# Interleaving the two heads of a block-diagonal attention tile over the partitions

## The chip, the cores and the metric

The kernel runs on one core of one Trainium2 chip. The metric is the device time of one execution in microseconds (us); a lower time is better. The core has five engines that matter here: PE (TensorE, matmul; PEld is its loading of weights), DVE (VectorE), ACT (ScalarE), POOL (GpSimd) and SP (SyncE, which issues most DMAs). Sixteen DMA engines carry out what SP and ACT issue.

## The reference, cut to what matters

```python
# B, H, S, D = 4, 8, 768, 64; chunks of 32 queries, 16 keys to the left, 8 to the right, 8 memory keys
q_c    = q[:, :, c_start:c_end]                           # 32 queries of a chunk
k_full = concatenate([mem_k, k[:, :, l_start:r_end]])     # 8 + 56 = 64 keys (fewer at the two ends of S)
v_full = concatenate([mem_v, v[:, :, l_start:r_end]])
scores = 0.125 * (q_c @ k_full.T);  scores -= max(scores)
a      = exp(scores);  a /= sum(a) + 1e-9
out[:, :, c_start:c_end] = a @ v_full
# then on all 3072 tokens, x is 3072 x 512:
h  = x @ w_in                                             # 512 x 1024
ln = layernorm(h * softmax(h)) * g_ln
x2 = ln @ w_out                                           # 1024 x 512
y  = leaky_relu(x2 @ w_in2, 0.01) @ w_out2                # 512 x 2048, 2048 x 512
```

## The kernel before, in words

The weights arrive as 64-bit floats, which the kernel decodes on the chip into pairs of float32 halves. The first 340 us or so hold attention and the first feed-forward layer; the rest holds the second one, which the change does not touch.

Attention works on 24 tiles of 128 tokens of one batch entry. A tile holds 8 heads, taken as 4 pairs (`hp`), and 4 chunks (`c`) of 32 tokens. For each pair and chunk one matmul computes the scores of both heads at once: the contraction runs over 128 partitions, 64 for each of the two heads, and the moving operand (`kbd`) is block diagonal. Its shape is `[128, 2, 4, 4, 64]`, where the second index `j` says for which head of the pair the 64 key columns are. For `j = 0` the lower 64 partitions hold the keys of head 0 and the upper 64 partitions hold zeros; for `j = 1` it is the other way round. The values (`vbd`) are laid out the same way, with 64 keys of each head on the partitions. The zeros are written once, by two memsets of a buffer, and the loads of all later tiles leave them alone. There are four such buffers: `kbd` and `vbd` (zeroed by DVE, used for tile 0 and for tiles 2 and on) and `k1` and `v1` (zeroed by POOL, used for tile 1 alone).

One tile goes through `s_scores` (16 matmuls, line 204; row maxima on DVE, lines 213 and 214), `s_exp` (8 ACT instructions of 128 x 64 into `p`, line 221), `s_pt` (4 transposes of 128 x 128 on PE, line 234, and a copy, line 238), `s_pv` (16 matmuls, line 246, and the division by the row sum, line 251), and `s_xt` (4 transposes, line 260, and the split into halves, lines 263 and 266). `s_h` and what follows is the first feed-forward layer (line 91 is the helper that records its matmuls, line 351 the second product).

Every load of `kbd` or `vbd` is two DMAs of 256 KB from SP (line 185), one for each `j`, with 64 partitions of 4 KB each. A load of `q` is one DMA of 256 KB over 128 partitions (line 179), a load of raw weights one DMA of 512 KB over 128 partitions (lines 97 and 99).

At the start SP issues loads in an order written out by hand, `LOADS` (w0 to w7 are the eight pieces of the first weight matrix, raw):

```python
LOADS = "q0 k0 w0 w1 k1 q1 w5 v0 w3 w2 v1 w7 w4 g w6".split()
STEPS = "a10100a10ab03a21b22a14a223b34353bbb55447564667656777"
```

`STEPS` is the order in which DVE, ACT and POOL take the steps of the first two tiles (`a`, `b`) and of the decoding of w0 to w7 (`0` to `7`). Line 109 is the first step of a decoding and waits for the raw weights. After that the framework's planner sets the order of the instructions on each engine by modelled times, until the second feed-forward layer, which is written out by hand again.

Of the kernel before, what the change touches and what calls it, by code (L numbers as in the profile page):

```python
# [9 lines left out]
F32 = mybir.dt.float32  # L10
F32R = mybir.dt.float32r
U32 = mybir.dt.uint32
AF = mybir.ActivationFunctionType
# [26 lines left out]
def tile_kernel(  # L40
# [13 lines left out]
    P = 128  # L54
# [12 lines left out]
    SCALE = 0.125  # L67
# [10 lines left out]
    ident = const.tile([P, P], F32, name="ident")  # L78
# [83 lines left out]
    p1 = satt.enter_context(tc.tile_pool(name="p1", bufs=1, side="right"))  # L162
# [2 lines left out]

    def kv_tile(pool, name, eng):
        t = pool.tile([P, 2, 4, 4, 64], F32, name=name)
        eng.memset(t[0:64, 1], 0.0)
        eng.memset(t[64:128, 0], 0.0)
        return t  # L170

    warm = sm.tile([P, 1], F32, name="warm")
    nc.scalar.activation(warm, mhalf, AF.Exp)
    kbd = kv_tile(p1, "kbd", nc.vector)
    vbd = kv_tile(p1, "vbd", nc.vector)

    def load_q(i):
# [3 lines left out]

    def load_kv(i, dst, src):
        for j in range(2):
            sl = slice(64 * j, 64 * j + 64)
            nc.sync.dma_start(
                out=dst[sl, j], in_=src[i, sl].rearrange("p (h c k) -> p h c k", h=4, c=4)
            )
        return dst

    def load_tile(i):  # L190
        return load_q(i), load_kv(i, kbd, kw), load_kv(i, vbd, vw)
# [7 lines left out]
    def s_scores(i, q, k):  # L199
        sc = ps_att.tile([P, 8, 64], F32, name="att")  # L200
        for hp in range(4):
            for c in range(4):
                cs = slice(32 * c, 32 * c + 32)
                nc.tensor.matmul(  # L204
                    sc[cs, 2 * hp : 2 * hp + 2, :], q[:, hp, cs], k[:, :, hp, c, :],
                    start=True, stop=True,
                )
        if i % TPB == 0:
            nc.vector.memset(sc[0:32, :, 8:24], NEG)
        if i % TPB == TPB - 1:  # L210
            nc.vector.memset(sc[96:128, :, 56:64], NEG)
        nms = sm.tile([P, 8], F32, name="nms")
        nc.vector.tensor_reduce(out=nms, in_=sc, op=ALU.max, axis=AX.X, negate=True)
        nc.vector.tensor_scalar_mul(nms, nms, SCALE)  # L214
        return sc, nms

    def s_exp(sc, nms):
        p = p1.tile([P, 8, 64], F32, name="p")
        rs = sm.tile([P, 8], F32, name="rs")
        for h in range(8):  # L220
            nc.scalar.activation(  # L221
                p[:, h], sc[:, h], AF.Exp, bias=nms[:, h : h + 1], scale=SCALE,
                accum_out=rs[:, h : h + 1],
            )
        return p, rs
# [5 lines left out]
    def s_pt(p):  # L231
        ptp = ps_tr.tile([P, 4, P], F32, name="tr")
        for hp in range(4):
            nc.tensor.transpose(
                ptp[:, hp], p[:, 2 * hp : 2 * hp + 2].rearrange("p h k -> p (h k)"), ident
            )
        pt = pa.tile([P, 4, P], F32, name="pt")
        nc.vector.tensor_copy(pt, ptp)
        return pt
# [120 lines left out]
    def att_steps(i, ld):  # L360
        sc, nms = s_scores(i, ld[0], ld[1])
        yield
        p, rs = s_exp(sc, nms)
        yield
        s_rs(rs)
        pt = s_pt(p)
        yield
        x = s_pv(pt, ld[2], rs)
        yield
        hl, low = s_xt(x)  # L370
        xs.append(hl)
        yield
        low()
        yield

    def w1_raw(u):
        hf, kk = divmod(u, KD)
        return load_raw(w1[kk * P : (kk + 1) * P, hf * 1024 : (hf + 1) * 1024], sraw)

    k1 = kv_tile(st, "k1", nc.gpsimd)  # L380
    v1 = kv_tile(st, "v1", nc.gpsimd)
    got = {}
    for d in LOADS:
        if d == "g":
            nc.sync.dma_start(out=g_sb, in_=g_ln.rearrange("(k p) -> p k", p=P))
            continue
        n = int(d[1])
        if d[0] == "q":
            got[d] = load_q(n)
        elif d[0] == "k":  # L390
            got[d] = load_kv(n, (kbd, k1)[n], kw)
        elif d[0] == "v":
            got[d] = load_kv(n, (vbd, v1)[n], vw)
        else:
            got[d] = w1_raw(n)
# [37 lines left out]
    for i in range(NTILE + 1):  # L433
        a = i + 2
        b, t = divmod(i, TB)
# [4 lines left out]
        if att:  # L440
            p, rs = s_exp(*s_scores(a, ld[0], ld[1]))
            s_rs(rs)
# [10 lines left out]
        if att:  # L453
            pt = s_pt(p)
        if so is not None:
            j = i - 1
# [34 lines left out]
    spx, sxr, sxt, sl, sr, sq, sd, sg, s4 = (ExitStack() for _ in range(9))  # L491
# [64 lines left out]
    for i in range(NTILE + 1, NTILE + LAG):  # L556
        j = i - LAG
# [211 lines left out]
    for n, (q, v) in enumerate(units):  # L769
# [8 lines left out]
        k = n - NA  # L778
# [51 lines left out]
    hp = s4.enter_context(tc.tile_pool(name="hp", bufs=2, side="right", reuse_waits="tile"))  # L830
# [24 lines left out]
    for n, (v, s, k) in enumerate(steps):  # L855
        h, l = halves.pop(n)
        if s == 0 and k == 0:
            acc = {c: [ps.tile([P, BT], F32, name=c) for e in range(2)] for c in "ABC"}
            A, B, C = (acc[c] for c in "ABC")
# [105 lines left out]
```

## Time and profile before

| what | value |
|---|---|
| median of 3 runs | 866.36 us (865.71 to 875.55) |
| profiled execution | 871.68 us, of which 869.9 us are the span from the first to the last instruction |
| mean granted TensorE clock | 0.994 of full speed |
| busy share of the span | PE 95%, PEld 76%, DVE 74%, ACT 54%, POOL 7% |
| DMA | 190.95 MB, mean 220 GB/s |

The profiled execution is 5.3 us longer than the median; sums made from the trace are set against the profiled one and then moved by that amount.

### The profile page before, as it was taken

The numbers are of one execution on the slowest core, as the hardware profiler recorded it, in microseconds if no ns is written. First come the engines' busy times: TensorE is split into PE (matmuls) and PEld (weight loads), VectorE is DVE, ScalarE is ACT, GpSimd is POOL, SyncE is SP. The second block draws the span as 40 slices with busy tenths as digits, with TensorE's granted clock in tenths as the row PEclk, the third lists the DMA queues.
The fourth block names the chain that finished last, engine by engine and source line by source line (L and its number), as shares of the span: only waits on it lengthen the run. The fifth ranks groups of instructions, "written<-read, shape, count | busy, mean of one in ns | idle before, by whom it ended". The sixth has DMA issues, their size and how long they took to land.

```text
span 869.9 us, 13633 instructions
## 1 busy us (share of the span) xinstructions
PE 827.6 (95%) x4960; PEld 658.1 (76%) x4960; DVE 643.4 (74%) x1145; ACT 472.2 (54%) x1067; POOL 56.6 (7%) x63
## 2 busy tenths in 40 slices
PE   3789999999999999996999999999999999999998
PEld 2457777777777778784887888788877888888886
DVE  4788986777877778758889843856579869758673
ACT  2477864455554544536556644677657535544541
POOL 2233420000000000000000000000000010010001
PEclk9999999999999999998999999999999999999999
DMA  8756777968697763572688756377777466646542
GB/s 227 180 161 195 206 204 227 282 198 260 201 287 226 234 212 140 194 269 88 244 324 325 281 222 236 139 289 294 269 287 282 146 221 206 198 161 227 197 145 97
DMA packets 69891, 190.95 MB, mean 220 GB/s; under 512 B 8000, under 2 KB 32064, under 8 KB 65856
## 3 DMA queue, kind: packets, MB, share of 16 engines
q1 hardware_dynamic: 56864, 175.14, 60.4%
q10 hardware_dynamic: 12960, 14.95, 5.5%
q8 instruction: 39, 0.64, 0.3%
q14 instruction: 28, 0.23, 0.1%
HBM read 129.24 MB, written 60.82 MB: 218 GB/s over the span
## 4 chain that ended last, share of the span: by engine, by line
PE 74%; DVE 12%; DMA 6%; ACT 4%; issue 2%; POOL 1%; SPq 0%; ACTq 0%; DVEq 0%; POOLq 0%
PE C L654 24%; PE B L654 14%; PE x2p L351 12%; PE A L654 10%; PE h L91 9%; DMA raw<-in_w 2%; PE att L246 2%; PE att L204 2%; DMA x2d<-x2s 1%; DMA ring<-gd 1%; DVE so L290 1%; ACT p L221 1%; DMA kbd<-in_kw 1%; DVE m L124 1%; PE tr L260 1%
## 5 line engine op out<-in xcount | busy, mean ns | idle before, releaser
L351 PE MATMUL x2p<-lhl,w2h 128*128 128x512 f32 x384 | 127.3, 406 | 0.5 <-ACT x2s L357 0.5
L654 PE MATMUL C<-xP,L 128*128 128x512 f32 x384 | 97.4, 395 | 7.5 <-ACT u L683 5.9
L654 PEld LDWEIGHTS C<-xP,L 128*128 128x128 f32 x384 | 72.4, 190 | 24.9 <-ACT u L683 6.7
L351 PEld LDWEIGHTS x2p<-lhl,w2h 128*128 128x128 f32 x384 | 70.1, 189 | 16.8 <-issue 2.0
L351 PE MATMUL x2p<-lhl,w2l 128*128 128x512 f32 x192 | 77.5, 404 | 0.0
L221 ACT ACTIVATE p<-att,nms 128x64 f32<-128x64 f32 x192 | 57.4, 322 | 23.5 <-DVE nms L214 23.4
L91 PE MATMUL h<-w1h,xh 128*128 128x512 f32 x168 | 68.7, 409 | 1.5 <-ACT w1h L133 1.5
L91 PE MATMUL h<-w1l,xh 128*128 128x512 f32 x168 | 67.5, 402 | 2.3 <-POOL w1l L134 2.3
L654 PE MATMUL C<-h,L 128*128 128x512 f32 x192 | 67.0, 390 | 0.0
L91 PE MATMUL h<-w1h,xl 128*128 128x512 f32 x168 | 66.7, 397 | 0.0
L765 DVE TENSOR_TENSOR ring<-ring,h 128x512 fp32r<-128x512 f32 x96 | 61.8, 685 | 3.7 <-ACT h L764 3.1
L680 ACT ACTIVATE g<-g 128x512 f32<-128x512 f32 x72 | 45.1, 627 | 26.0 <-DVE g L699 20.0
L295 ACT ACTIVATE e<-so,nmu 128x1024 f32<-128x1024 f32 x24 | 27.7, 1154 | 57.1 <-DVE nmu L293 56.6
L764 ACT ACTIVATE h<-ring 128x512 fp32r<-128x512 f32 x72 | 39.8, 621 | 31.7 <-DMA ring<-gd 22.8
L654 PE MATMUL B<-xP,L 128*128 128x512 f32 x192 | 49.7, 395 | 0.2 <-DVE g L709 0.2
L699 DVE TENSOR_TENSOR g<-B,u 128x512 f32<-128x512 f32 x23 | 15.9, 690 | 42.2 <-PE B L654 42.2
L764 ACT ACTIVATE h<-t2k 128x512 fp32r<-128x512 f32 x48 | 28.7, 628 | 33.1 <-DVE t2k L757 18.6
L654 PEld LDWEIGHTS B<-xP,L 128*128 128x128 f32 x192 | 36.5, 191 | 8.6 <-DVE g L709 0.6
L351 PEld LDWEIGHTS x2p<-lhl,w2l 128*128 128x128 f32 x192 | 36.2, 189 | 7.8 <-issue 1.0
L654 PEld LDWEIGHTS C<-h,L 128*128 128x128 f32 x192 | 36.0, 188 | 7.9 <-DVE u L879 0.4
L221 ACT ACTIVATION_READ_ACCUMULATOR p<-att,nms 128x1 f32 x192 | 41.3, 215 | 0.0
L91 PEld LDWEIGHTS h<-w1h,xh 128*128 128x128 f32 x168 | 31.8, 189 | 11.6 <-issue 3.2
(183 smaller groups left out, 1908.3 us busy)
## 6 DMA issues: line engine op xcount, KB each, us to landing
ring<-gd SPq DMA_DIRECT2D x48, 768.0 KB, 4.0
gd<-g SPq DMA_DIRECT2D x24, 1024.0 KB, 5.1
raw<-in_w SPq DMA_DIRECT2D x32, 512.0 KB, 5.3
L<-w3f SPq DMA_DIRECT2D x14, 896.0 KB, 4.7
kbd<-in_kw SPq DMA_DIRECT2D x46, 256.0 KB, 4.6
vbd<-in_vw SPq DMA_DIRECT2D x46, 256.0 KB, 4.3
lnd<-sl SPq DMA_DIRECT2D x16, 512.0 KB, 3.4
lt<-lnd ACTq DMA_DIRECT2D x64, 128.0 KB, 2.8
```

The lines of the kernel that those rows point to most:

```text
L91: nc.tensor.matmul(ps, a, b, start=(i == 0), stop=(i == 3 * n - 1))
L124: nc.vector.scalar_tensor_tensor(out=mu, in0=raw[:, :, 1], scalar=0x80000000, in1=mu, op0=ALU.bitwise_and, op1=ALU.bitwise_or,)
L204: nc.tensor.matmul(sc[cs, 2 * hp : 2 * hp + 2, :], q[:, hp, cs], k[:, :, hp, c, :], start=True, stop=True,)
L221: nc.scalar.activation(p[:, h], sc[:, h], AF.Exp, bias=nms[:, h : h + 1], scale=SCALE, accum_out=rs[:, h : h + 1],)
L246: nc.tensor.matmul(xp[cs, 2 * hp : 2 * hp + 2, :], pt[:, hp, cs], v[:, :, hp, c, :], start=True, stop=True,)
L295: nc.scalar.activation(e, so, AF.Square, bias=nmu, accum_out=ve)
L351: nc.tensor.matmul(ps, a[:, kk, es], r[:, kk], start=(kk == 0 and n == 0), stop=(kk == KF - 1 and n == 2),)
L654: nc.tensor.matmul(acc, w[i], x[j], start=first and n == 0, stop=last and n == 2, skip_group_check=True)
L680: nc.scalar.activation(u.g[:, i], u.g[:, i] if src is None else src, AF.Prelu, alpha=0.01)
L699: tt(out=o.g[:, 1], in0=o.acc["B"], in1=o.u2, op=ALU.add)
L764: nc.scalar.activation(h[:, i], src[n_], AF.Copy)
L765: tt(out=l[:, i], in0=src[n_], in1=h[:, i].bitcast(F32), op=ALU.subtract)
```

## The change

The two heads of a pair no longer take the lower and the upper 64 partitions but every second partition each. The host prepares `q`, `k` and `v` in that order of rows. A load for `j` writes partitions `j, j+2, j+4, ...` and reads every second 4 KB row of the source. The memsets zero the whole of a buffer, as an engine's operand has consecutive partitions. For the values the contraction runs over the keys of both heads, so the probabilities have to be interleaved too: `p` becomes `[128, 4, 64, 2]`, and each `exp` writes its 64 results with a step of two elements. The transposes read 128 consecutive elements as before.

```diff
     def kv_tile(pool, name, eng):
         t = pool.tile([P, 2, 4, 4, 64], F32, name=name)
-        eng.memset(t[0:64, 1], 0.0)
-        eng.memset(t[64:128, 0], 0.0)
+        eng.memset(t[:, 0], 0.0)
+        eng.memset(t[:, 1], 0.0)
         return t
...
         for j in range(2):
-            sl = slice(64 * j, 64 * j + 64)
             nc.sync.dma_start(
-                out=dst[sl, j], in_=src[i, sl].rearrange("p (h c k) -> p h c k", h=4, c=4)
+                out=dst[j::2, j], in_=src[i, j::2].rearrange("p (h c k) -> p h c k", h=4, c=4)
             )
...
-        p = p1.tile([P, 8, 64], F32, name="p")
+        p = p1.tile([P, 4, 64, 2], F32, name="p")
...
-                p[:, h], sc[:, h], AF.Exp, bias=nms[:, h : h + 1], scale=SCALE,
+                p[:, h // 2, :, h % 2], sc[:, h], AF.Exp, bias=nms[:, h : h + 1], scale=SCALE,
...
-                ptp[:, hp], p[:, 2 * hp : 2 * hp + 2].rearrange("p h k -> p (h k)"), ident
+                ptp[:, hp], p[:, hp].rearrange("p k j -> p (k j)"), ident
...
-    kw = windows(k, mk).transpose(0, 3, 2, 6, 1, 4, 5).reshape(B * nt, 128, -1)
-    vw = windows(v, mv).transpose(0, 3, 2, 5, 1, 4, 6).reshape(B * nt, 128, -1)
-    qt = q.reshape(B, 4, 2, nt, 128, D).transpose(0, 3, 2, 5, 1, 4).reshape(B * nt, 128, -1)
+    kw = windows(k, mk).transpose(0, 3, 6, 2, 1, 4, 5).reshape(B * nt, 128, -1)
+    vw = windows(v, mv).transpose(0, 3, 5, 2, 1, 4, 6).reshape(B * nt, 128, -1)
+    qt = q.reshape(B, 4, 2, nt, 128, D).transpose(0, 3, 5, 2, 1, 4).reshape(B * nt, 128, -1)
```

## Rows read from the trace of the kernel before

**Rows 1.** The page's first part: busy time and share of each engine.
```profile
PE 827.6 (95%) x4960; PEld 658.1 (76%) x4960; DVE 643.4 (74%) x1145; ACT 472.2 (54%) x1067; POOL 56.6 (7%) x63
```

**Rows 2.** Windows: length, busy time of each engine, PEclk, DMA share, GB/s.
```profile
0.00:25.00 25.00, 8.79 (x104) 5.97 (x104) 11.18 (x21) 6.62 (x23) 5.71 (x12) 1.00 0.91 229
25.00:60.00 35.00, 27.57 (x240) 17.29 (x240) 28.95 (x55) 20.36 (x71) 10.67 (x9) 1.00 0.62 167
60.00:340.00 280.00, 275.83 (x2373) 214.03 (x2374) 222.99 (x489) 160.13 (x515) 30.98 (x35) 1.00 0.74 220
```

**Rows 3.** Waits of PE, 60 to 340 us: total, times, longest.
```profile
PE tr L234 <- ACT p L221: 1.9, 3, 1.0
```

**Rows 4.** Chain of waits, 0 to 60 us: start, length, what.
```profile
3.03 8.55 DMA raw<-in_w
11.60 13.12 DMA raw<-in_w
...
25.30 2.47 ACT p L221 x16
...
44.14 2.18 ACT p L221 x14
```

**Rows 5.** Timeline, 0 to 28 us: start, length, engine, instruction.
```profile
1.00 0.91 DVE L168 MEMSET kbd<- 64x1024 f32 x1 [1.00 <-PEq L952]
1.18 1.18 SPq L185 DMA_DIRECT2D kbd<-in_kw  x2
2.17 0.91 DVE L169 MEMSET kbd<- 64x1024 f32 x1 [0.25 <-issue]
2.24 0.95 POOL L169 MEMSET k<- 64x1024 f32 x1
2.40 1.06 SPq L97 DMA_DIRECT2D raw<-in_w  x2
...
3.50 1.51 SPq L185 DMA_DIRECT2D k<-in_kw  x2
...
4.51 0.91 DVE L169 MEMSET vbd<- 64x1024 f32 x1 [0.25 <-issue]
...
7.08 1.23 SPq L185 DMA_DIRECT2D vbd<-in_vw  x2
```

**Rows 6.** Timeline of SP, 36 to 80 us: issues of DMAs.
```profile
40.44 1.10 SPq L185 DMA_DIRECT2D kbd<-in_kw  x2
...
42.22 0.90 SPq L97 DMA_DIRECT2D raw<-in_w  x2
```

**Rows 7.** Windows of the DMA rate; the last two columns are DMA share and GB/s.
```profile
5.00:9.00 4.00, 1.73 (x32) 1.51 (x32) 0.42 (x1) 0.00 (x0) 0.17 (x1) 1.00 0.92 281
9.00:25.00 16.00, 7.06 (x76) 4.47 (x72) 7.53 (x17) 5.13 (x21) 1.27 (x1) 1.00 1.04 243
25.00:29.00 4.00, 2.59 (x6) 1.23 (x6) 2.26 (x5) 3.77 (x19) 0.15 (x1) 1.00 1.02 302
42.75:43.75 1.00, 0.86 (x3) 0.36 (x3) 1.00 (x2) 0.00 (x0) 1.00 (x1) 1.00 1.12 258
44.75:47.25 2.50, 2.02 (x11) 1.28 (x10) 2.43 (x5) 2.39 (x14) 0.33 (x1) 1.00 1.04 413
```

**Rows 8.** ACT's groups, 0 to 60 us: busy us, mean ns.
```profile
L221 ACT ACTIVATE p<-att,nms 128x64 f32<-128x64 f32 x32 | 9.6, 331 | 2.4 <-DVE nms L214 2.4
...
L109 ACT ACTIVATE m<-raw 128x512 f32<-128x512 f32 x10 | 6.4, 659 | 17.5 <-DMA raw<-in_w 17.5
L133 ACT ACTIVATE w1h<-m 128x512 fp32r<-128x512 f32 x8 | 5.1, 640 | 6.9 <-DVE m L124 6.9
...
L285 ACT ACTIVATE e<-h,hnm 128x1024 f32<-128x1024 f32 x1 | 1.1, 1117 | 3.7 <-DVE hnm L282 3.7
```

**Rows 9.** DMA issues, 60 to 340 us: count, KB each, us to landing.
```profile
vbd<-in_vw SPq DMA_DIRECT2D x40, 256.0 KB, 4.1
kbd<-in_kw SPq DMA_DIRECT2D x38, 256.0 KB, 4.5
```

## The prediction

> **What bounds the kernel now.** I read the page's first part, then cut the stretch that the change can reach (0 to 340 us) into windows, then took the waits of PE and the chain of waits in the part where PE is not full. PE is busy for 827.6 us of 869.9 [rows 1]. The windows show where the missing time is: from 60 to 340 us PE has 275.8 us of work in 280, and its longest entry among the waits there is 1.9 us in all [rows 2, 3]. In that stretch a faster or slower load, exp or memset is worth nothing as long as it stays hidden. The first 60 us are different: PE has 8.8 us of work in the first 25 us and 27.6 in the next 35 [rows 2]. The chain of waits runs through the DMAs of raw weights from 3.03 to 24.7 us [rows 4], and in those 25 us the DMA engines are busy at a share of 0.91 [rows 2]. From 25 to 60 us DVE is the fullest engine, with 28.95 us of 35 [rows 2]; it works off what the late weights left undone. So whatever moves the loads of the first 25 us moves the end of the kernel by about as much, and hardly anything else in the change can.
>
> **The transfers.** The change leaves the number of DMAs and their bytes alone and spreads each transfer of 64 rows over all partitions. What such a transfer costs now can be read where few others are in flight. At 40.44 us SP issues the two halves of a `kbd` load, then `q`, and at 42.22 us two raw weights over 128 partitions [rows 6]. While the second half of `kbd` is moved (42.75 to 43.75) the DMA engines are fully busy and move 258 GB/s; while the weights are moved (44.75 to 47.25) they are as busy and move 413 GB/s [rows 7]. Both have rows of 4 KB, so the 64 rows in one half of the partitions are what differs. I read it as a limit on the side of the partitions: half of them take data at some 0.6 of the rate of all. The first 25 us contain the keys and values of two tiles, 8 transfers of 256 KB, beside 8 raw weights of 512 KB and 2 `q` of 256 KB (26 x 262 KB = 6.8 MB), and there the rate is 281 GB/s from 5 to 9 us and 243 GB/s from 9 to 25 us at a share of 1.04; from 25 to 29 us, with weights at the end of the list, it is 302 [rows 7]. The slow rate holds for weights queued among the keys and values too, as one transfer that holds up an engine holds up what is behind it.
>
> The sum: 16.0 us at 243 GB/s are 3.89 MB. At 302 GB/s, the rate of the window after, they take 12.9 us, a gain of 3.1 us; at 413 GB/s, the best window, 9.4 us, a gain of 6.6 us; if the rate stays, nothing. I take 3.1 us: the window from 25 to 29 us is the nearest to the one in question, under the same load from the start of the list. It is not certain that the new layout reaches all of the partitions' capacity at any one moment, since one engine's rows are now neighbours at a step of two. The ends stay in the range. What is late next after the weights is DVE's decoding, which has 11.2 us of work in the first 25 us and so has room to take it earlier [rows 2].
>
> The Trainium skill (SBUF — State Buffer, section "Door 1: The DMA port swizzle") says that partitions 0 to 63 reach only 8 of 16 ports, 64 to 127 the other 8, and that a transfer over all of them reaches 16, at 196 against 328 GB/s for 1 MiB; the trace agrees in kind, with 258 against 413 GB/s [rows 7]. By its map the new transfers touch all 16 ports; that result, full rate, is the second case below.
>
> From 60 us on, the loads lie beside other work: the DMA share is 0.74 [rows 2], and PE does not wait for them. There the same gain costs and brings nothing.
>
> **The memsets.** Today the loads of `kbd` write other bytes than the memsets, and SP issues them at 1.18 us while the first memset is still running (1.00 to 1.91) [rows 5]. After the change the memset of `j` covers the bytes that the load of `j` writes, so load 0 can be issued only after 1.91 us (it was at 1.18) and load 1 only after 2.17 + 0.91 = 3.08 us (it was at about 1.77): 0.7 and 1.3 us later. Behind them on SP stand all other loads, the first raw weights (issued at 2.40) among them, so the list moves by 1.3 us. No other buffer adds to this: POOL's memset of `k1` ends at 3.19 us and its load is issued at 3.50, DVE's last one of `vbd` ends at 5.42 us and its load is issued at 7.08 [rows 5], each to be issued later still. A memset has 1024 elements in each partition as before; over 128 partitions instead of 64 I take the same 0.91 us (no row shows it; at most twice, which would add 0.9 + 0.9 us to the start; less is excluded, as the elements of a partition stay as many). DMAs are not issued in that gap and the engines run dry, so the 1.3 us count in full, unless the loads that follow catch up, which is the term above.
>
> **The exp.** Each of 192 exps writes 64 elements with a step of two. The nearest row is an ACT read with that step: line 109 takes every second word of the raw weights and needs 659 ns for 512 elements, where line 133 reads consecutive ones in 640 [rows 8]. That is 0.04 ns an element, 2 ns an exp. The other end is a write at half rate: lines 285 and 133 differ by 477 ns for 512 elements, 0.93 ns each [rows 8], so 60 ns more on 331. In the start the chain holds 30 exps of ACT [rows 4], which would make 1.8 us; after 60 us they lie beside PE, and ACT has 160 us of work in 280 there [rows 2]. I take 0, by the nearer row; less than before is excluded, since the elements stay as many. The transposes read the same 128 consecutive elements and wait for the same two exps. The matmuls read the same columns; which rows are zero does not change their number, so they cost nothing.
>
> **The sum.** -3.1 (loads) + 1.3 (memsets) + 0 (exp) = -1.8 us: 871.7 - 1.8 = 869.9 us for the profiled execution. The profile is 5.3 us above the median of the runs, so 866.4 - 1.8 = 864.6 us. That is 0.2%, far within the 2% that a measurement of this kernel can tell from no change.
>
> **The rivals.**
> - All transfers at full rate. For it: 413 GB/s at 44.75 us [rows 7]. Against: even at 25 to 29 us, with weights alone at the head of the list, only 302 were reached. It gives -6.6 + 1.3 = -5.3 us, 861.1 us.
> - The wait for the memset takes the place of a gain that does not come. If every transfer still fills only half of the partitions' capacity at a time, or if it is the source that limits, the rate stays at 243 GB/s and the list only starts later: +1.3 us, 867.7 us. It decides as soon as the rate from 9 to 25 us stays under 3.89 MB / (16.0 - 1.3) us = 265 GB/s. For it: 243 and 258 GB/s are what is seen behind any key or value load, and the trace does not show a transfer with a step.
> - The source reads cost more. Each transfer now reads every second row of 4 KB from memory instead of 256 KB in a row. If this slows the transfer, the stretch behind 60 us decides: 78 such transfers [rows 9] of 262 KB / 258 GB/s = 1.02 us are 79 us of the 0.74 x 280 = 207 us of DMA work [rows 2], and the other 128 us stay. The DMA engines are full when a transfer takes (280 - 128) / 78 = 1.95 us, 1.9 times as long; from there PE waits. At 100 GB/s (2.6 us each) the stretch takes 128 + 204 = 332 us, 52 more: 918 us. Against it: rows of 4 KB are the unit on the other side in either case.
> - The planner orders the engines otherwise, because a wait or a cost in its model moved. PE has 4.2 us of slack from 60 to 340 us [rows 2], so this can take some 2 to 4 us either way, 862 to 869 us.
> - The exp at half rate with the forecast for the rest: -1.8 + 1.8, 866.4 us.
>
> **How the numbers follow.** Forecast (net -0.5 to -3.5 us) 0.42; full rate 0.18; the wait without gain (+0.5 to +2 us) 0.27; slow source 0.03; another order 0.06; slow exp 0.04. The likeliest gives 864.6 us. The range takes in full rate at the low end and the wait without gain at the high end, with half a microsecond for the spread of medians: 860.6 to 868.3 us. Faster by over 2% would need 17 us, more than all the chain's time in DMAs could give back: 0.01. Slower by over 2% is the slow source, with a little for what I do not see: 0.04. Within 2%: 0.95.
>
> **What the profile after would show.** Windows of the second half of a `kbd` load well above 258 GB/s, and the stretch from 9 us to the end of the first list above 265. The load of `kbd` issued behind DVE's memsets, at about 1.9 and 3.1 us, and the first raw weights at 3.7. The first long wait of ACT's line 109 ending near 11 to 13 us, the last near 23 instead of 24.7. The exp within 10 ns of 331. PE's windows after 60 us unchanged. The prediction is wrong if the DMA rate at the start does not move, if a `kbd` load takes longer than 1 us a half, or if PE gains waits after 60 us.

## The result, and the profile after

The changed kernel takes 862.43 us (median of 8 runs, 860.33 to 864.25). The kernel before, run beside it 8 times, takes 871.07 us (865.71 to 875.55); its first three runs, on which the prediction was based, had a median of 866.36. The ratio is 0.9899, with a 95% interval of 0.9873 to 0.9924: 1.0% faster, some 8.8 us. The sign of the forecast is right, but the gain is about five times the 1.8 us that were forecast. The time lies in the predicted range, 860.6 to 868.3 us, and that is partly luck: forecast and range were counted from 866.36 us. Counted from 871.07, the same steps would have given 869.3 us and a range of 865.3 to 873.0, and 862.43 would have been below it. The profiled spans are 869.9 and 861.4 us, 8.5 us apart, so the trace shows the whole of the gain.

Windows of the changed kernel, with the columns of [rows 2] and [rows 7]:

```profile
0.00:25.00 25.00, 12.65 (x147) 8.21 (x148) 17.48 (x34) 12.38 (x44) 8.11 (x14) 1.00 0.92 334
25.00:60.00 35.00, 29.53 (x267) 20.07 (x267) 30.35 (x63) 21.64 (x73) 12.75 (x10) 1.00 0.43 139
60.00:340.00 280.00, 276.30 (x2341) 214.44 (x2340) 222.46 (x483) 156.64 (x497) 26.48 (x31) 1.00 0.67 220
...
5.00:9.00 4.00, 1.94 (x32) 1.51 (x32) 0.14 (x1) 0.85 (x2) 0.00 (x0) 1.00 0.97 315
9.00:25.00 16.00, 10.71 (x115) 6.70 (x116) 13.84 (x30) 10.04 (x41) 3.82 (x3) 1.00 1.00 376
...
33.50:34.50 1.00, 0.55 (x2) 0.48 (x3) 1.00 (x2) 0.00 (x0) 1.00 (x2) 1.00 0.96 350
```

The DMA engines are as busy as before in the first 25 us (0.92 against 0.91) but move 334 GB/s instead of 229, and from 9 to 25 us 376 instead of 243 [rows 2, 7]. DVE gets 17.5 us of work done there instead of 11.2. The last line covers most of the second half of an isolated `kbd` load: 350 GB/s, where [rows 7] have 258. From 60 us on PE is as full as before (276.3 us of 280); the DMA share fell from 0.74 to 0.67 for the same 220 GB/s, which brings nothing there.

Timeline of the changed kernel, all engines, 0 to 28 us:

```profile
1.00 0.91 DVE L168 MEMSET kbd<- 128x1024 f32 x1 [1.00 <-PEq L951]
1.16 0.42 SPq L97 DMA_DIRECT2D raw<-in_w  x1
...
1.94 1.55 SPq L184 DMA_DIRECT2D kbd<-in_kw  x2
...
2.08 0.91 DVE L169 MEMSET kbd<- 128x1024 f32 x1 [0.16 <-issue]
...
3.53 0.59 SPq L97 DMA_DIRECT2D raw<-in_w  x1
...
8.15 1.22 ACT L109 ACTIVATE m<-raw 128x512 f32<-128x512 f32 x2 [5.93 <-DMA raw<-in_w]
...
14.83 0.68 ACT L109 ACTIVATE m<-raw 128x512 f32<-128x512 f32 x1 [0.48 <-DMA raw<-in_w]
...
16.07 0.67 ACT L109 ACTIVATE m<-raw 128x512 f32<-128x512 f32 x1 [0.56 <-DMA raw<-in_w]
```

A memset of 128 partitions takes the same 0.91 us as one of 64 [rows 5], and the loads of `kbd` do wait for the two memsets (issued from 1.94 us). But SP does not stand still meanwhile: at 1.16 us it issues a piece of raw weights, which used to come after both `kbd` loads, at 2.40 us [rows 5]. `LOADS` is unchanged; the planner has moved the piece ahead. It can, because the block that fixes the order at the start (`manual_schedule`) names DVE, ACT and POOL, and not SP. The decoding of the first weights starts at 8.15 us where the chain in [rows 4] has 11.60, and the wait for the fourth piece of weights (`w2`) ends at 16.07 us, where that chain has 24.72. In what follows, "the last early wait" is this one. The chain of waits of the changed kernel no longer runs through raw weights:

```profile
3.02 3.87 DMA kbd<-in_kw
7.02 1.97 PE att L203 x32
...
10.27 1.89 ACT p L220 x12
...
35.46 2.18 ACT p L220 x14
```

The x14 at 35.46 us counts each exp twice, as the instruction itself and as the read of its row sum that follows it:

```profile
35.46 0.32 ACT L220 ACTIVATE p<-att,nms 128x64 f32<-128x64 f32 x1 [2.38 <-DVE nms L213]
35.67 0.19 ACT L220 ACTIVATION_READ_ACCUMULATOR p<-att,nms 128x1 f32 x1
```

These seven exps are those that stand at 44.14 us in [rows 4]: 8.7 us earlier. The end is 8.5 us earlier, so all of the gain is made by then and carried to the end.

ACT's groups from 0 to 60 us: an exp takes 333 ns on average (331 in [rows 8]).

```profile
L220 ACT ACTIVATE p<-att,nms 128x64 f32<-128x64 f32 x40 | 12.0, 333 | 3.3 <-DVE nms L213 3.3
...
L109 ACT ACTIVATE m<-raw 128x512 f32<-128x512 f32 x10 | 6.5, 666 | 8.4 <-DMA raw<-in_w 8.4
L133 ACT ACTIVATE w1h<-m 128x512 fp32r<-128x512 f32 x8 | 5.1, 640 | 6.7 <-DVE m L124 6.7
```

The wait of line 109 for raw weights fell from 17.5 to 8.4 us.

### The profile page after: what moved, and what is told of

Read it like the earlier page. It is cut to its first block, busy times and chain, and to the rows that moved or that the text cites. A ratio compares the mean times of both kernels' runs of the same rounds, so it can differ in the third digit from the quotient of the medians.

```text
span 861.4 us, 13637 instructions
## 1 busy us (share of the span) xinstructions
PE 825.6 (96%) x4960; PEld 657.3 (76%) x4960; DVE 643.6 (75%) x1145; ACT 472.3 (55%) x1067; POOL 56.4 (7%) x63
## 4 chain that ended last, share of the span: by engine, by line
PE 75%; DVE 13%; ACT 4%; DMA 4%; issue 2%; POOL 1%; ACTq 0%; DVEq 0%; POOLq 0%
PE C L653 24%; PE B L653 13%; PE x2p L350 12%; PE h L91 10%; PE A L653 10%; PE att L203 2%; PE att L245 2%; DMA x2d<-x2s 1%; DMA ring<-gd 1%; DVE so L289 1%; DMA kbd<-in_kw 1%; PE tr L233 1%; DVE m L124 1%; ACT p L220 1%; PE tr L259 1%
```

## The experiments

The theory: a load of 64 rows is slow when its partitions all lie on one side of partition 64, and the gain is what the first two tiles' loads give back at the start. The rivals: the way in which the source is read; the new order of the first loads; the loads of all the later tiles; the exps. Each ratio is to runs of the kernel before on the same chip, and a gain in us is worked out from it; the two medians can lie 1 or 2 us further apart.

**1. The memsets alone.** The kernel before, with

```diff
-        eng.memset(t[0:64, 1], 0.0)
-        eng.memset(t[64:128, 0], 0.0)
+        eng.memset(t[:, 0], 0.0)
+        eng.memset(t[:, 1], 0.0)
```

> The kernel before with the whole buffers zeroed; the loads stay in two halves. The first load of keys then waits for its memset, and the planner issues one piece of raw weights ahead of it. Theory (the partitions that a load reaches set the rate): no gain, the rate from 9 to 25 us stays near 243 GB/s, the time is that of before, at most 1.3 us longer. Rival (the new order of the first loads is the gain): some 8 us shorter.

Measured: 866.79 us against 872.65, ratio 0.9949 (0.9925 to 0.9973), some 4.4 us less. Neither expectation had that number: there is a gain, about half of the whole, without any change to a transfer. The planner issues the first weights ahead of the keys here too, and the rate from 9 to 25 us is 285 GB/s:

```profile
9.00:25.00 16.00, 10.82 (x106) 6.47 (x99) 10.55 (x22) 9.00 (x39) 2.13 (x2) 0.87 1.05 285
```

**2. Every second partition, source in a row.** The changed kernel, with the keys and values laid out by the host as before and

```diff
-                out=dst[j::2, j], in_=src[i, j::2].rearrange(...)
+                out=dst[j::2, j], in_=src[i, 64 * j : 64 * j + 64].rearrange(...)
```

> The changed kernel with keys and values read from memory as 256 KB in a row, still written to every second partition. Theory (partitions): as fast as the changed kernel, about 8.5 us below before, 350 GB/s or more from 12 to 25 us. Rival (the source rows with a step are the gain): as slow as before.

Measured: 861.98 us, ratio 0.9906 (0.9874 to 0.9937), as fast as the changed kernel.

```profile
9.00:25.00 16.00, 10.79 (x110) 6.80 (x114) 13.92 (x28) 10.30 (x42) 3.83 (x3) 0.97 0.99 373
```

**3. Source with a step, halves of the partitions.** The kernel before, with the host layout of the changed one for keys and values and

```diff
-                out=dst[sl, j], in_=src[i, sl].rearrange(...)
+                out=dst[sl, j], in_=src[i, j::2].rearrange(...)
```

> The kernel before, with every second row of 4 KB read from memory, written to one half of the partitions. The order of all engines is that of before. Theory (partitions): as slow as before, within 0.3%, about 243 GB/s from 9 to 25 us. Rival (source): about 8.5 us shorter.

Measured: 871.91 us, ratio 1.0013 (0.9978 to 1.0048): the time of before.

```profile
9.00:25.00 16.00, 6.78 (x72) 4.34 (x72) 6.70 (x16) 4.86 (x20) 1.27 (x1) 1.00 1.04 218
```

Experiments 2 and 3 together settle the side: the partitions that are written count, and not how the source is read. In one profiled run each, the source with a step is even a little slower (218 against 243 GB/s), which the times don't show.

**4. Sixty-four partitions in a row, across the middle.** The changed kernel, with

```diff
-                out=dst[j::2, j], in_=src[i, j::2].rearrange(...)
+                out=dst[32:96, j], in_=src[i, j::2].rearrange(...)
```

> The changed kernel with every load of keys and values written to partitions 32 to 95, one after the other (the other partitions keep their zeros, so the attention uses the wrong keys and values). If what counts is that a load reaches both sides of partition 64, it is as fast as the changed kernel, 8 to 9 us below before, and a half of a load moves at about 400 GB/s. If what counts is a step between the partitions, or that half of them are left out, it is as slow as before, at 240 to 260 GB/s.

Measured: 862.18 us, ratio 0.9904 (0.9869 to 0.9939).

```profile
9.00:25.00 16.00, 11.07 (x102) 6.84 (x106) 13.61 (x28) 10.79 (x42) 3.83 (x3) 0.89 1.01 382
```

So it is neither the step between the partitions nor that half of them are left out: 64 partitions in a row do as well as every second one, if they lie on both sides of partition 64. A half of a load by itself did not reach the 400 GB/s that were expected; while the isolated `kbd` load of this run is moved, from 34 to 35 us, the rate is 332 GB/s, near the 350 of the changed kernel.

**5. The order of the first loads alone.** The kernel before, with

```diff
-LOADS = "q0 k0 w0 w1 k1 q1 w5 v0 w3 w2 v1 w7 w4 g w6".split()
+LOADS = "q0 w0 k0 w1 k1 q1 w5 v0 w3 w2 v1 w7 w4 g w6".split()
```

> The kernel before with one piece of raw weights issued ahead of the first keys, and nothing else: no memset, no layout changes. The kernel with whole memsets was 0.5% faster than before. If the new order of the first loads did that, this one is some 4 us below before too. If it was the pause that the wait puts between the first loads, it is as slow as before.

Measured: 866.94 us, ratio 0.9952 (0.993 to 0.9974), some 4.2 us less. That is the gain of experiment 1, without a memset or a wait: the order did it. (The planner also changes PE's order in one place, here as in experiment 1: ten matmuls of the second tile's scores go ahead of the first tile's last transpose, at 14.3 us.) The decoding starts earlier than before and the stretch from 9 to 25 us is faster (295 against 243 GB/s), though each transfer of keys or values still goes to one side:

```profile
10.25 1.21 ACT L109 ACTIVATE m<-raw 128x512 f32<-128x512 f32 x2 [8.03 <-DMA raw<-in_w]
...
20.58 0.66 ACT L109 ACTIVATE m<-raw 128x512 f32<-128x512 f32 x1 [1.37 <-DMA raw<-in_w]
```

```profile
9.00:25.00 16.00, 10.99 (x110) 6.64 (x103) 10.00 (x22) 9.00 (x39) 1.59 (x2) 0.92 1.04 295
...
13.50:16.00 2.50, 2.39 (x21) 1.25 (x24) 2.35 (x6) 1.52 (x8) 0.00 (x0) 1.00 1.03 229
16.50:18.50 2.00, 1.78 (x38) 1.34 (x31) 0.86 (x2) 0.00 (x0) 0.92 (x1) 1.00 1.03 404
18.50:21.50 3.00, 1.45 (x20) 0.78 (x12) 1.52 (x3) 1.59 (x5) 0.00 (x0) 1.00 1.04 235
```

The rate alternates here: it is 229 to 235 GB/s in some stretches and 404 in the one between, which is near the 413 of weights by themselves [rows 7]. In the kernel before it is 229 from 13.5 to 16 us, 267 from 18.5 to 21, and between them

```profile
16.50:18.00 1.50, 1.50 (x32) 1.10 (x23) 0.28 (x1) 0.07 (x1) 1.27 (x1) 1.00 1.01 240
```

The trace keeps 16 landings of each DMA, and there the two kernels differ: those of `w2`, the piece of the last early wait, spread from 19.93 to 24.72 us in the kernel before and from 18.43 to 20.55 us here. A likely reading, which no experiment tests: in the kernel before the DMA engines are at different places in the list, so that some of them always work on keys or values; here they come to the weights together and move them at full rate.

**6. The reach alone.** The kernel before, with

```diff
-        eng.memset(t[0:64, 1], 0.0)
-        eng.memset(t[64:128, 0], 0.0)
+        eng.memset(t[0:32], 0.0)
+        eng.memset(t[96:128], 0.0)
...
-                out=dst[sl, j], in_=src[i, sl].rearrange(...)
+                out=dst[32:96, j], in_=src[i, sl].rearrange(...)
```

No load waits for a memset, and every engine has its instructions in the order of before.

> The kernel before with the loads of keys and values written to partitions 32 to 95, and with memsets of partitions 0 to 31 and 96 to 127, which the loads don't touch (the attention uses the wrong keys and values). Every engine keeps the order of before, and no load waits for a memset. If the reach over both sides of partition 64 suffices by itself, 8 to 9 us below before; if it adds to what the order brings, about 4 us below before. The DMA rate from 9 to 25 us is above 350 GB/s either way.

Measured: 862.56 us, ratio 0.9902 (0.987 to 0.9934), some 8.5 us less.

```profile
9.00:25.00 16.00, 9.16 (x82) 5.51 (x82) 13.16 (x28) 10.67 (x42) 3.06 (x3) 1.00 1.02 379
```

```profile
10.87 1.21 ACT L109 ACTIVATE m<-raw 128x512 f32<-128x512 f32 x2 [8.65 <-DMA raw<-in_w]
...
17.82 0.66 ACT L109 ACTIVATE m<-raw 128x512 f32<-128x512 f32 x1 [0.57 <-DMA raw<-in_w]
```

The memsets here fill twice as many elements of each partition and take 1.76 us each, but no load waits for them. The reach by itself brings all of the gain that the times can show. The two effects don't add: 4.4 and 8.5 us each by itself, 8.8 us together. In the trace the order still brings something on top, as the last early wait ends at 17.82 us here and at 16.07 in the changed kernel, but the intervals of the two ratios cover each other.

**7. The first two tiles alone.** The changed kernel, with every later load written to one half of the partitions:

```diff
-                out=dst[j::2, j], in_=...
+                out=dst[slice(j, None, 2) if i < 2 else slice(64 * j, 64 * j + 64), j], in_=...
```

> The changed kernel, but from the third tile on the loads are written to one half of the partitions each (later tiles use keys and values out of place). Theory (only the first 25 us count): as fast as the changed kernel within 1 us, though the transfers after 60 us are slow again. Rival (the loads of all tiles count): between the two, near the kernel with whole memsets alone, 866 to 867 us.

Measured: 864.62 us, ratio 0.9915 (0.9881 to 0.9949). The changed kernel's 0.9899 lies in that interval; the median is 2.2 us above 862.43, more than the 1 us I had allowed. Part of that can be the start: SP issues the third tile's loads at 17.49 and 18.99 us here, so slow transfers still lie in the first 25 us. The next wait for weights ends later than in the changed kernel (there at 21.12 us), and the exps that stand there at 35.46 us come at 36.68:

```profile
22.60 0.67 ACT L109 ACTIVATE m<-raw 128x512 f32<-128x512 f32 x1 [2.12 <-DMA raw<-in_w]
```

The span of this profiled run is nonetheless 860.6 us, 0.8 less than the changed kernel's. From 60 to 340 us the DMA share is 0.73 at 221 GB/s, against 0.67 in the changed kernel, while PE's work is the same 276.3 us:

```profile
60.00:340.00 280.00, 276.32 (x2344) 214.52 (x2343) 222.95 (x483) 155.82 (x498) 26.70 (x32) 1.00 0.73 221
```

**8. All tiles but the first two.** The kernel before, with the source read with a step and the same expression turned round (`i >= 2`).

> The kernel before with every second partition for the loads from the third tile on only (those tiles use keys and values out of place); the first two are loaded as before. Theory (only the first 25 us count): the time of before, at most 1 us less. Rival (the loads of all tiles count): at least 3 us less.

Measured: 871.5 us against 871.6, ratio 0.9999 (0.9977 to 1.0022). Forty-four of the 48 pairs of transfers are fast here, and nothing is gained.

**9. The exps alone.** The kernel before, with `p` as `[P, 4, 64, 2]`, the exps written with a step of two and the transposes reading that layout.

> The kernel before with the exps written with a step of two and the transposes reading that layout; keys, values and loads as before (so the values meet probabilities in the wrong order). Theory (the step of two costs ACT nothing): an exp at 320 to 335 ns, the time of before within 0.3%. Rival (a write at half rate): 380 ns an exp, some 2 us longer.

Measured: 870.56 us, ratio 0.9983 (0.9957 to 1.001), no difference. All engines have the order of before, and an exp takes 324 ns in the middle of 192 values, where before it was 320 (the first line):

```profile
L221 ACT ACTIVATE p<-att,nms x192: 293/320/367, 12.7 to 331.4; 128x64 f32<-128x64 f32 x192
...
L221 ACT ACTIVATE p<-att,nms x192: 297/324/369, 13.1 to 332.0; 128x64 f32<-128x64 f32 x192
```

**10. The first keys zeroed by two engines.** The changed kernel, with the second memset of `kbd` on POOL.

> The changed kernel with the second memset of the first key buffer on POOL, so that both halves of the first keys can be issued at about 1.9 us. If the wait for the memsets still costs something, up to 1 us less than the changed kernel (861 to 862 us where that has 862.4); if it is hidden behind the weights issued first, no difference.

Measured: 861.79 us, ratio 0.9903 (0.9875 to 0.9932), the same as the changed kernel's 0.9899. What is left of the wait for the memsets costs nothing that can be seen. PE has the order of the kernel before in this run, so the matmuls that the planner moved in the changed kernel are not its gain either.

**11. Both first weights ahead of the first keys.** The changed kernel, with

```diff
-LOADS = "q0 k0 w0 w1 k1 q1 w5 v0 w3 w2 v1 w7 w4 g w6".split()
-STEPS = "a10100a10ab03a21b22a14a223b34353bbb55447564667656777"
+LOADS = "q0 w1 w0 k0 k1 q1 w5 v0 w3 w2 v1 w7 w4 g w6".split()
+STEPS = "1010010aaab03a21b22a14a223b34353bbb55447564667656777"
```

> The changed kernel with both first weights loaded ahead of the first keys, and DVE and ACT decoding them before they turn to the first tile's scores. DVE is idle for some 4 us before the first scores in the changed kernel. If DVE's work of decoding is what the start now waits for, 1 to 3 us less than the changed kernel; if the first tile's attention is, no difference or up to 1 us more.

Measured: 863.2 us, ratio 0.9924 (0.9898 to 0.9951): no gain. The two weights that the changed kernel waits for until 14.83 and 16.07 us are there without a wait, and the end is no earlier:

```profile
14.55 1.37 ACT L109 ACTIVATE m<-raw 128x512 f32<-128x512 f32 x2
```

The chain of waits runs through the load of the first keys, until 8.46 us, and then through the first tile's attention and DVE, no longer through weights. No version tried beats the changed kernel by more than its spread.

## Why the prediction was right in sign and small in size

**Where the change can act: right.** Only the first 25 us count. Experiment 8 makes the transfers of all tiles but the first two fast and gains nothing, experiment 7 makes those of the first two fast and keeps at least most of the gain, and the chain is 8.7 us earlier by the exps at 35.46 us and 8.5 us at the end.

**What limits the transfers: right.** The prediction read 258 against 413 GB/s as a limit on the side of the partitions. Experiments 2, 3, 4 and 6 show it: the destination counts, the source doesn't, and both layouts tried that have as many partitions on either side of partition 64 are fast. The Trainium skill's map (SBUF — State Buffer, section "Door 1: The DMA port swizzle") gives partitions 0 to 63 one set of 8 ports and 64 to 127 the other, so that 32 to 95 reach all 16; the 382 and 379 GB/s of experiments 4 and 6 agree with it.

**The size of that term: wrong.** The step that failed is "At 302 GB/s, the rate of the window after, they take 12.9 us, a gain of 3.1 us". The window at 25 to 29 us was no stand-in for fast transfers. The values of the second tile were still landing (their two DMAs, issued at 13.1 and 14.6 us, took 12.9 and 12.5 us to land), so slow transfers were in it. And the load of `g`, which moves its 1024 numbers one by one, shows in it: 1062 packets of the window (the first line) are smaller than 512 bytes, against 170 in the 16 us before (the second).

```profile
DMA packets 1388, 1.21 MB, mean 302 GB/s; under 512 B 1062, under 2 KB 1062, under 8 KB 1387
...
DMA packets 1183, 3.89 MB, mean 243 GB/s; under 512 B 170, under 2 KB 170, under 8 KB 1183
```

The rate became 376 GB/s, near the best window's 413. At 376 the sum's 3.89 MB take 10.3 us, a gain of 5.7 instead of 3.1; the stretch between the first wait of line 109 and the last early one did shrink by 5.2 us, from 13.1 to 7.9. The other 3.45 us of the 8.7 (the first wait ended at 8.15 instead of 11.60) lie ahead of the stretch that I summed, and the transfers do not bring them alone: in experiment 6, with the order of before, that wait ends at 10.87, and the stretch is 6.2 us shorter (13.1 to 6.95). By experiment 6, in which only the reach and the length of the memsets change, the term is 8.5 us in place of 3.1 by the times, and 7.8 by the profiled spans (869.9 and 862.1). The prediction expected the first long wait of line 109 to end at 11 to 13 us and the last near 23; both came much earlier.

**The memsets: wrong in sign.** The step "Behind them on SP stand all other loads, the first raw weights (issued at 2.40) among them, so the list moves by 1.3 us" took SP's order as fixed. The waits came where they were foreseen (1.94 us), but the planner put weights into the gap. In place of +1.3 us the memsets and the order brought 4.4 us less by themselves (experiment 1, and 5 for the order alone), and no difference that the times show beside fast transfers (the changed kernel against experiment 6). The prediction had another order as a rival, with 2 to 4 us from PE's side later on; it was SP's order at the start that moved.

**The exps, and the transfers after 60 us: right.** An exp takes 333 against 331 ns, with a ratio of 0.9983 for the step alone, and PE has 276.3 us of work from 60 to 340 us where it had 275.8. One reading was wrong but not needed: the "30 exps" of the chain count each exp with the read of its sum, as above, so they are 15, and the exp at half rate would have cost 0.9 us there and not 1.8.

**The rivals.** The slow source fell with experiment 3, the slow exp with experiment 9. The wait without gain fell on both its parts. The full rate was nearly the case that came. Its 861.1 us lie close to the measured 862.43 by luck: it stands for a gain of 5.3 us, not 8.8, and the low base of 866.36 made up for the rest. Its 6.6 us, too, left out the stretch before 9 us, and its 1.3 us for the memsets had the wrong sign. Another order came as well, but at the start, where that rival did not look for it.

**What stays open.** With slow transfers, one piece of weights ahead of the first keys raises the rate from 243 to 295 GB/s (experiment 5). The parts of a DMA land closer together there, but why that order keeps them so is not shown, and no experiment changes this alone. Whether the later tiles' slow transfers cost part of the 2.2 us of experiment 7 isn't settled either; the interval allows none.

## What to carry to other kernels

Lay a transfer of 64 partitions over both sides of partition 64; every second one and 32 to 95 did equally well here. Where a start is bound by loads, what is queued among such transfers gains with them: the weights here were laid out as before, and the last early wait for them ended 6.9 us earlier by the reach alone. Price such a gain over the whole stretch up to the last landing that something waits for, at a rate from a window that holds none of the slow transfers and no load of single words. And before charging a new wait to everything behind it, ask who sets the order of that queue: here a planner filled the gap, and the new order was worth more than the wait.

## What the runs showed of the hardware that was not expected

The kernel before spreads by 10 us from run to run (865.71 to 875.55 us, and 864 to 879 in experiments 3 and 9, which keep its order and its slow transfers), the changed one by 4 us (860.33 to 864.25).

In experiment 5 TensorE's granted clock was 0.50, its lower level of 1.2 GHz, from 25 to 29 us, and 1.00 again from 33 us, after a stretch in which PE had 2.7 of 4 us and 2.6 of 4 us of work; in the kernel before it was 1.00 in all of these windows, with 1.4 and 2.7 of 4 us in the same stretch. Experiment 6 shows such a drop too (0.57 from 25 to 29 us). Experiment 5's windows, around the drop:

```profile
17.00:21.00 4.00, 2.73 (x39) 1.93 (x36) 2.15 (x4) 1.09 (x2) 0.42 (x1) 1.00 1.06 302
21.00:25.00 4.00, 2.57 (x6) 1.28 (x7) 2.43 (x5) 3.60 (x19) 0.32 (x1) 0.69 1.05 327
25.00:29.00 4.00, 3.00 (x21) 1.71 (x24) 3.93 (x8) 1.86 (x3) 2.24 (x2) 0.50 1.06 273
29.00:33.00 4.00, 4.00 (x33) 3.03 (x26) 2.04 (x5) 0.63 (x1) 1.27 (x1) 0.53 0.61 154
33.00:37.00 4.00, 3.78 (x43) 2.17 (x42) 3.25 (x6) 1.71 (x3) 0.00 (x0) 1.00 0.00 1
```

DVE is the fuller engine from 25 to 29 us (3.93 of 4 us), but from 29 to 33 us PE is full, and the chain of waits runs through PE from 28.23 to 33.0 us. From the second tile's exps (21.14 us) to the next in the chain (40.82) it takes 19.7 us, where the kernel before takes 18.8 (25.30 to 44.14), so the drop can have cost up to some 0.8 us. The granted clock does not tell the whole pace of PE at the start: in the kernel before, where it is 1.00, 32 matmuls of one kind take 1.94 us at 20.62 and 1.08 us at 32.41.

```profile
20.62 1.94 PE L246 MATMUL att<-vbd,pt 128*32 128x128 f32 x32 [2.57 <-DMA vbd<-in_vw]
32.41 1.08 PE L246 MATMUL att<-v,pt 128*32 128x128 f32 x32 [1.00 <-DVE pt L238]
```
